# The diagonal of the scores by a select, and a new order of 2000 steps, in a recurrent attention and mixture-of-experts kernel

## Chip, cores and metric

The kernel runs on one core of a Trainium2 chip. The metric is the device time in microseconds (us) of one execution; smaller is better. Times of the trace are counted from the start of its span. TensorE (PE), VectorE (DVE), ScalarE (ACT) and GpSimd (POOL) each work through an instruction queue of their own in order; SP issues most of the DMA transfers, in order as well.

## The reference

Three layers follow each other. The first is a recurrence over 768 time steps with a state of 48x48 for each of 4 batches and 8 heads, the second a feed-forward layer with a softmax and a layer norm between its products, and the third a top-1 mixture of 8 experts.

```python
for t in range(S):                       # S = 768
    cur = np.einsum('bhd,bhe->bhde', u[None] * kt, vt)
    y[:, :, t] = np.einsum('bhd,bhde->bhe', rt, state + cur)
    state = wt[:, :, :, None] * state + np.einsum('bhd,bhe->bhde', kt, vt)
...
h = x @ w_in                             # x: 3072 x 384, w_in: 384 x 1024
solu = h * softmax(h)
ln = (solu - mu) / np.sqrt(var + 1e-06) * g_ln
x = ln @ w_out                           # 1024 x 384
...
expert_idx = np.argmax(x @ w_gate, axis=1)
out[mask] = gate_w[mask, None] * (np.maximum(x[mask] @ w1[e], 0.0) @ w2[e])
```

The term with `u` is the share of the current time step: a number for each token and head, the sum over d of r * u * k.

## The kernel before

The 3072 tokens are cut into 24 units (6 chunks of 128 time steps, for each of 4 batches). In a unit the recurrence becomes products of matrices.

- `plan_T` prepares a unit: it transposes w, r and k on TensorE (`transposes`, L686), takes running products of the decay on VectorE (L700), their inverse on ScalarE (ln and exp, L710 and L712) with a Newton step on GpSimd (`tq` L717, `newt` L721 and L722), and scales r and k with them (`rt` L705, `kt` L727). The diagonal of the scores comes from r * u * k (`ru`, L732 and L733, GpSimd), its sum per head (`a0`, L738, VectorE, 128x8) and `dg` (L743, GpSimd), which spreads the eight sums of a token on the diagonals of eight 128x128 matrices, the tile `am` of 128x1024.
- `plan_A` transposes the scaled k back (`back`, L795, and a copy on ScalarE, L800), makes the scores (L762), copies them under the causal mask over `am` (L766, the diagonal stays as `dg` left it), multiplies with the state and with v (L780), copies the result x into a high and a low half (L785, L788) and brings the state forward (L807, L813, L815, L820).
- `plan_M` is the first product of the MLP with its softmax and norm (L186, L187 and L189; each product is made of three, with high and low halves of both factors), `plan_C` transposes and `plan_O` makes the second product. The MLP of a unit runs seven units behind its attention (LAG = 7); M0 means unit 0's first product, T7 the preparation of unit 7, and so on.
- Before M0 the weights w_in (six pieces of 128x512) and w_out (eight of 128x384) are turned from 64-bit words into 32-bit floats on the chip: load (L221), three steps of integers on VectorE (L226, L228, L229), two checks on ScalarE (L235, L236), a copy as the high half on ScalarE (L243), and the rest as the low half on GpSimd (L244). `prep_gate` folds w_out with the gate's weights (L256, L259, L263), and the result is split as the gate columns (L267 on ScalarE, L268 on VectorE); M0's output takes the same PSUM banks that these columns lay in.
- `gate_steps` picks the expert of each token, and an indirect DMA on GpSimd (L958) scatters the rows into `xsd`, sorted by expert. The experts then work in eight jobs of fixed size: SP gathers rows (L1235), TensorE transposes them (L1244), ScalarE and VectorE split them (L1246, L1247), and both layers of the expert follow (L186 to L189, L1253, L1254, L195). Weights are split into halves on ScalarE and GpSimd (L1046, L1047). The result goes out by an indirect DMA (L1273).

Nothing is issued at once: `at(t, fn)` puts each step on a list, and when all 2000 are there, `emit` runs them in the order of the tuple `_ORDER`, a permutation written out at the head of the file:

```python
def emit():
    steps = sorted(plan, key=lambda x: (x[0], x[1]))
    assert len(steps) == len(_ORDER)
    for q in _ORDER:
        steps[q][2]()
```

A step issues one or several instructions, mostly on one engine; so `_ORDER` sets the order of the queue of each engine and of SP, and nothing else does. A wait of an instruction holds all that stand behind it on its engine. Loads of units have three buffers each (NB = 3): the load of unit 9's w waits until unit 6's transposes have read it.

Some steps by their number: 351 `newt` of T6; 359 `ru` of T7; 353 `kt` of T6; 362 `back` of unit 6; 377 the k transposes of T7; 255 the last L263; 358 the scores of unit 6; 384 its L807; 378 its L780; 408 the r transposes of T8; 381 the copy of x of unit 6 (L785); 341, 345 and 357 the three ScalarE steps of the last piece of w_in (L235, L236, L243); 388 and 389 the gate columns (L267, L268); 392 M0; 395 and 396 the loads of unit 9's w and r; 452 the load of unit 10's v.

Of the kernel before, what the change touches and what calls it, by code (L numbers as in the profile page):

```python
# [13 lines left out]
ALU = mybir.AluOpType  # L14
# [105 lines left out]
def rwkv_moe_kernel(ctx: ExitStack, tc: tile.TileContext, r, k, v, w, u, w_in, w_out, g_ln, w_gate, w1, w2, out, dbg=None):  # L120
    nc = tc.nc
# [566 lines left out]
    def plan_T(i, t, mode):  # L688
# [52 lines left out]
        def dg():  # L741
            u["am"] = aw2.tile([128, 2, 4, 128], F32, tag="am", name="am")
            nc.gpsimd.tensor_tensor(  # L743
                out=u["am"].rearrange("p q a t -> p (q a) t"), in0=ident.rearrange("p (o t) -> p o t", o=1).to_broadcast([128, H, 128]),
                in1=u["a0"].rearrange("p q (a o) -> p (q a) o", o=1).to_broadcast([128, H, 128]), op=ALU.mult)
# [647 lines left out]
```

## Time and profile before

| | before |
|---|---|
| device time, three runs | 671.34, 671.69, 673.26 us (median 671.69) |
| the profiled execution, its own time | 671.95 us |
| its span in the trace | 670.04 us |
| busy: TensorE, VectorE, ScalarE, GpSimd | 626.2, 358.8, 340.1, 386.9 us |
| mean granted clock of TensorE | 0.965 |

A span is the time from the first to the last instruction of the trace; what lies between it and the execution's own time is ahead of or behind it. The execution has four stages: the start, 0 to 97 us, in which the weights are prepared and seven units of attention run ahead; the mixed stretch of attention and MLP, 97 to 430; a short change-over at 430 to 440; and the experts, from there to 670. [...]

### The profile page before, as it was taken

The page shows a single profiled execution, that of the slowest core. Times are in us where ns is not written, and L with a number is a line of the kernel's source. Part 1 is how long each engine was busy: PE and PEld are TensorE (multiplying, and loading weights), DVE is VectorE, ACT ScalarE, POOL GpSimd, SP SyncE. Part 2 cuts the span into 40 slices and gives each one's busy share as a digit, 9 for nine tenths or more (in the row PEclk, how much of TensorE's full clock was granted, in tenths as well). Part 3 has the DMA queues.
Part 4 walks back from the last instruction along what each step waited for, and adds up shares of the span by engine and source line. Part 5 has one row for each costly group of instructions (what it writes and reads, how often), then busy time and mean ns, then how long its engine had stood idle before and what let it go on. Part 6 is the DMA issues. An engine that isn't in the chain of part 4 may idle for free. (4 is left out here: it accounts for less than half of the span.)

```text
span 670.0 us, 13443 instructions
## 1 busy us (share of the span) xinstructions
PE 626.2 (93%) x5143; PEld 569.4 (85%) x5143; DVE 358.8 (54%) x876; ACT 340.1 (51%) x711; POOL 386.9 (58%) x389
## 2 busy tenths in 40 slices
PE   5768689999999999999999999799999999999993
PEld 5657568888888888888888899798999999999993
DVE  7989866785776777686656675432122211131220
ACT  3756645565665555565447785154533534354330
POOL 7888867755369576646600453243756486475541
PEclk8878969999999999999999999989999999999998
DMA  8955611366134122530103121364444455534401
GB/s 194 232 135 127 154 36 36 96 195 198 36 94 109 49 61 48 131 72 25 38 1 102 60 99 51 107 187 151 144 153 131 154 150 166 166 113 152 129 11 35
DMA packets 125103, 72.56 MB, mean 108 GB/s; under 512 B 104071, under 2 KB 115836, under 8 KB 125029
## 3 DMA queue, kind: packets, MB, share of 16 engines
q1 hardware_dynamic: 121749, 62.13, 34.6%
q0 software_dynamic: 3280, 9.47, 3.8%
q8 instruction: 43, 0.70, 0.4%
q14 instruction: 31, 0.25, 0.1%
HBM read 55.79 MB, written 16.29 MB: 108 GB/s over the span
## 5 line engine op out<-in xcount | busy, mean ns | idle before, releaser
L1254 DVE SCALAR_TENSOR_TENSOR hl<-bank,hh 128x384 fp32r<-128x384 f32 (+5 forms) x70 | 37.1, 551 | 112.5 <-ACT hh L1253 103.4
L1047 POOL TENSOR_TENSOR wbl<-stg,wbh 128x768 fp32r<-128x768 f32 x32 | 59.0, 1852 | 36.5 <-ACT wbh L1046 36.3
L195 PE MATMUL bank<-wbh,hh 128*128 128x384 f32 (+4 forms) x216 | 73.7, 341 | 0.0
L195 PE MATMUL bank<-wbl,hh 128*128 128x384 f32 (+4 forms) x216 | 72.6, 336 | 0.0
L186 PE MATMUL bank<-xth,wah 128*128 128x384 f32 (+5 forms) x210 | 71.1, 344 | 0.0
L187 PE MATMUL bank<-xtl,wah 128*128 128x384 f32 (+5 forms) x210 | 69.9, 338 | 0.0
L186 PE MATMUL bank<-wbh,lh 128*128 128x392 f32 x192 | 67.8, 353 | 0.3 <-ACT xo L870 0.3
L1253 ACT ACTIVATE hh<-bank 128x384 fp32r<-128x384 f32 (+5 forms) x70 | 33.1, 490 | 66.0 <-PE bank L189 56.8
L187 PE MATMUL bank<-wbl,lh 128*128 128x392 f32 x192 | 65.2, 340 | 0.0
L1047 POOL TENSOR_TENSOR wal<-stg,wah 128x1024 fp32r<-128x1024 f32 x24 | 57.5, 2407 | 11.6 <-ACT wah L1046 11.4
L717 POOL TENSOR_TENSOR tq<-qe,yq 128x512 f32<-128x512 f32 x24 | 29.1, 1212 | 60.7 <-ACT yq L712 49.8
L1273 POOL DMA_INDIRECT out_dram<-yo,xg x28 | 27.6, 985 | 56.9 <-ACT yo L1270 37.4
L743 POOL TENSOR_TENSOR am<-ident,a 128x1024 f32<-128x1024 f32 x24 | 46.1, 1919 | 4.1 <-DVE a L738 2.8
L189 PE MATMUL bank<-xth,wal 128*128 128x384 f32 (+5 forms) x210 | 47.9, 337 | 0.0
L958 POOL DMA_INDIRECT xsd<-xo,ai x24 | 24.3, 1011 | 37.6 <-DMA xsd<-xo,ai 13.1
L186 PE MATMUL pair<-wah,wah 128*128 128x512 f32 x102 | 42.0, 411 | 2.5 <-DVE wbl L268 2.2
L395 DVE TENSOR_TENSOR ll<-bank,lh 128x512 fp32r<-128x512 f32 x48 | 32.6, 684 | 20.7 <-ACT lh L391 19.1
L195 PE MATMUL bank<-wbh,hl 128*128 128x384 f32 (+4 forms) x216 | 42.1, 336 | 0.0
L186 PEld LDWEIGHTS bank<-xth,wah 128*128 128x128 f32 x210 | 40.3, 192 | 1.3
L187 PEld LDWEIGHTS bank<-xtl,wah 128*128 128x128 f32 x210 | 40.3, 192 | 1.1
L187 PE MATMUL pair<-wal,wah 128*128 128x512 f32 x102 | 40.6, 398 | 0.0
L358 ACT ACTIVATE cc<-s,nmu 128x1024 f32<-128x1024 f32 x24 | 27.6, 1149 | 25.5 <-DVE nmu L356 25.3
(236 smaller groups left out, 1664.6 us busy)
## 6 DMA issues: line engine op xcount, KB each, us to landing
stg<-in_moe_w_dram SPq DMA_DIRECT2D x32, 384.0 KB, 3.3
stg<-in_moe_w_dram SPq DMA_DIRECT2D x24, 512.0 KB, 4.0
xsd<-zrow SPq DMA_DIRECT2D x16, 386.0 KB, 4.7
xg<-xsd SPq DMA_DIRECT2D x24, 193.0 KB, 2.8
lw<-in_w_dram SPq DMA_DIRECT2D x24, 192.0 KB, 3.5
lr<-in_r_dram SPq DMA_DIRECT2D x24, 192.0 KB, 4.1
lk<-in_k_dram SPq DMA_DIRECT2D x24, 192.0 KB, 3.7
lv<-in_v_dram SPq DMA_DIRECT2D x24, 192.0 KB, 3.3
```

What stands on the lines that cost most here:

```text
L186: nc.tensor.matmul(o, ah, bh, start=(i == 0), stop=False)
L187: nc.tensor.matmul(o, ah, bl, start=False, stop=False)
L189: nc.tensor.matmul(o, al, bh, start=False, stop=(i == n - 1))
L195: nc.tensor.matmul(o, a, b, start=(i == 0), stop=(i == len(seq) - 1))
L358: nc.scalar.activation(out=u["cc"], in_=u["s"], func=AF.Identity, bias=u["nmu"])
L395: yield 1.05 + 0.55 * g, lambda g=g, gs=gs: nc.vector.tensor_tensor(out=u["ll"][:, gs, :], in0=lp[g], in1=u["lh"][:, gs, :].bitcast(F32), ...
L717: nc.gpsimd.tensor_tensor(out=u["tq"], in0=u["qe"][:, :, 1:129], in1=u["yq"], op=ALU.mult)
L743: nc.gpsimd.tensor_tensor(out=u["am"].rearrange("p q a t -> p (q a) t"), in0=ident.rearrange("p (o t) -> p o t", o=1).to_broadcast([128, H ...
L1047: at(t + c1, lambda: eng.tensor_tensor(out=dl(), in0=u["st"], in1=dh().bitcast(F32), op=ALU.subtract))
L1253: at(t + d1, lambda: nc.scalar.activation(out=P2["h", 0][:, f, cs], in_=hp, func=AF.Relu))
L1254: at(t + d2, lambda: nc.vector.scalar_tensor_tensor(out=P2["h", 1][:, f, cs], in0=hp, scalar=0.0, in1=P2["h", 0][:, f, cs].bitcast(F32), o ...
L1273: nc.gpsimd.indirect_dma_start(out=out, out_offset=bass.IndirectOffsetOnAxis(ap=xg(j, i)[0:n, XW - 1:XW].bitcast(I32), axis=0), in_=box["y ...
```

## The change

`dg` no longer multiplies the identity with the sums. It selects: where the column t equals the partition, the sum is taken, elsewhere a zero is written. The operation reads one input (`a0`, broadcast along t) instead of two and stays on GpSimd:

```diff
         def dg():
             u["am"] = aw2.tile([128, 2, 4, 128], F32, tag="am", name="am")
-            nc.gpsimd.tensor_tensor(
-                out=u["am"].rearrange("p q a t -> p (q a) t"), in0=ident.rearrange("p (o t) -> p o t", o=1).to_broadcast([128, H, 128]),
-                in1=u["a0"].rearrange("p q (a o) -> p (q a) o", o=1).to_broadcast([128, H, 128]), op=ALU.mult)
+            nc.gpsimd.affine_select(
+                out=u["am"].rearrange("p q a t -> p (q a) t"), in_=u["a0"].rearrange("p q (a o) -> p (q a) o", o=1).to_broadcast([128, H, 128]),
+                pattern=[[0, H], [1, 128]], compare_op=ALU.is_equal, fill=0.0, base=0, channel_multiplier=-1)
         at(o("a0") + 0.1, dg)
```

All of `_ORDER` is replaced by another permutation of the same 2000 numbers; 1862 of them stand in another place, most by a few places, step 395 by 183. Some of the lines with the steps named above:

```diff
 _ORDER = (
...
-    91, 277, 155, 279, 230, 258, 282, 263, 235, 278, 310, 248, 280, 298, 290, 303, 207, 395, 253, 313, 200, 320, 170, 259, 295, 234, 308, 177, 336,
...
-    222, 329, 326, 276, 266, 268, 342, 352, 344, 351, 288, 355, 285, 356, 353, 291, 297, 269, 287, 349, 226, 227, 302, 232, 361, 377, 328, 311, 350,
-    312, 314, 363, 241, 315, 301, 255, 366, 362, 289, 370, 318, 376, 358, 321, 375, 384, 365, 408, 367, 378, 330, 335, 341, 332, 346, 383, 381, 398,
-    345, 450, 382, 357, 374, 388, 161, 389, 360, 392, 385, 379, 364, 380, 386, 402, 401, 409, 112, 410, 404, 400, 411, 111, 416, 333, 413, 414, 403,
...
+    222, 351, 226, 329, 344, 355, 359, 227, 285, 232, 352, 291, 297, 301, 287, 241, 363, 200, 368, 374, 349, 302, 255, 371, 366, 353, 372, 356, 328,
+    449, 362, 311, 377, 450, 350, 373, 312, 314, 318, 321, 376, 388, 315, 358, 397, 370, 365, 384, 339, 332, 333, 367, 378, 346, 375, 330, 383, 408,
+    381, 335, 341, 345, 389, 382, 357, 379, 360, 392, 385, 364, 361, 380, 386, 402, 401, 111, 400, 410, 404, 409, 112, 411, 416, 144, 166, 413, 403,
+    414, 61, 407, 420, 445, 424, 167, 417, 415, 387, 390, 437, 393, 428, 441, 429, 217, 419, 425, 423, 218, 422, 426, 452, 434, 427, 421, 395, 369,
+    455, 396, 442, 439, 430, 433, 459, 405, 438, 440, 431, 454, 467, 468, 456, 446, 457, 462, 500, 469, 406, 460, 436, 483, 435, 484, 472, 443, 391,
...
```

On each queue this makes, around the end of the start and behind it: on TensorE, 362 directly behind 255 and ahead of 377 (before: 377, 255, 362), and 378 ahead of 408 (before behind it); on ScalarE, 388 ahead of the last steps of the weights (before behind 357), and 381 ahead of 341 (before behind it); on GpSimd, 351 ahead of 359 (before behind it); on VectorE, the last integer step of the fourth piece of w_in ahead of 353 (before behind it); on SP, the load of the fifth piece of w_in ten places earlier, and 395 and 396 fifteen and eight places later, now behind 452. In the experts' change-over the first hidden layers of job 0 are issued ahead of the transposes of job 1. After M2 the queue of TensorE is the same but for shifts of a few places.

## Rows read from the trace of the kernel before

**Rows 1.** Windows by stage: length, busy us (instructions) by engine, PEclk, DMA share, GB/s.

```profile
0.00:97.00 97.00, 69.47 (x847) 59.79 (x848) 80.51 (x142) 54.31 (x127) 77.05 (x102) 0.84 0.63 148
97.00:430.00 333.00, 331.60 (x3008) 293.15 (x3007) 230.04 (x636) 190.21 (x417) 180.66 (x211) 1.00 0.30 79
430.00:440.00 10.00, 5.92 (x30) 5.03 (x29) 1.70 (x6) 1.79 (x4) 0.97 (x1) 0.74 0.74 236
440.00:657.00 217.00, 217.00 (x1251) 209.54 (x1251) 46.55 (x93) 93.22 (x163) 127.23 (x75) 1.00 0.43 135
```

**Rows 2.** Windows: the end of the start.

```profile
80.00:97.00 17.00, 11.55 (x117) 9.87 (x118) 13.36 (x22) 9.49 (x24) 10.42 (x9) 0.69 0.18 51
```

**Rows 3.** The waits of TensorE, 410 to 450 us: us in total, times, longest.

```profile
PE bank L1244 <- DMA xg<-xsd: 4.1, 2, 3.2
```

**Rows 4.** Lines of GpSimd, 0 to 97 us: count, busy us, mean ns, idle before.

```profile
L743 POOL TENSOR_TENSOR am<-ident,a 128x1024 f32<-128x1024 f32 x7 | 13.8, 1972 | 0.8 <-PE bank L780 0.8
```

**Rows 5.** Durations of three lines, 0 to 97 us, ns min/median/max.

```profile
L743 POOL TENSOR_TENSOR am<-ident,a x7: 1889/1891/2342, 16.3 to 68.6; 128x1024 f32<-128x1024 f32 x7
...
L721 POOL TENSOR_SCALAR tq<-tq x8: 617/797/1058, 12.0 to 90.6; 128x512 f32<-128x512 f32 x8
...
L226 DVE TENSOR_SCALAR t<-stg x14: 341/872/2053, 5.2 to 84.9; 128x384 int32<-128x384 int32 x8, 128x512 int32<-128x512 int32 x6
```

**Rows 6.** Timeline at 14 us: start, length, engine, line, operation, tiles.

```profile
14.09 1.00 POOL L732 TENSOR_TENSOR ru<-lr,ub 128x384 f32<-128x384 f32 x1
14.20 1.30 DVE L229 SCALAR_TENSOR_TENSOR a<-stg,a 128x384 uint32<-128x384 uint32 x1
```

**Rows 7.** Lines of GpSimd, whole run: a select and the smallest copy.

```profile
L140 POOL TENSOR_SCALAR_AFFINE_SELECT ident<-onesf 128x128 f32<-128x128 f32 x1 | 0.3, 283 | 0.0
...
L872 POOL COPY xo<-tokid 128x1 int32<-128x1 int32 x24 | 4.3, 187 | 0.1
```

**Rows 8.** Timeline of TensorE, 84 to 97 us; in brackets the idle time before.

```profile
84.47 1.11 PE L686 MATMUL bank<-ident,lk 128*128 128x128 f32 x4 [2.41 <-DVE kt L727]
...
85.38 1.29 PE L263 MATMUL pair<-wgt,wT 128*128 128x8 f32 x6
...
86.52 1.09 PE L795 MATMUL bank<-ident,kt 128*128 128x128 f32 x4
...
90.58 1.12 PE L686 MATMUL bank<-ident,lr 128*128 128x128 f32 x4
...
92.90 1.30 PE L780 MATMUL bank<-am,lv 128*32 128x128 f32 x32
...
96.41 0.50 PE L186 MATMUL pair<-wah,wah 128*128 128x512 f32 x1 [2.20 <-DVE wbl L268]
```

**Rows 9.** The timeline of GpSimd, VectorE and ScalarE, 76 to 96 us.

```profile
76.24 1.34 POOL L733 TENSOR_TENSOR ru<-ru,lk 128x384 f32<-128x384 f32 x1
...
80.25 1.24 DVE L226 TENSOR_SCALAR t<-stg 128x512 int32<-128x512 int32 x1 [0.88 <-DMA stg<-in_moe_w_in_dram]
...
84.34 0.68 DVE L229 SCALAR_TENSOR_TENSOR a<-stg,a 128x512 uint32<-128x512 uint32 x1
...
94.29 0.48 ACT L785 CAST wah<-bank 128x384 fp32r<-128x384 f32 x1 [4.97 <-PE bank L780]
...
95.89 0.21 ACT L267 CAST wbh<-pair 128x64 fp32r<-128x64 f32 x1
```

**Rows 10.** The timeline of TensorE in the gap, 437 to 439 us.

```profile
437.60 0.90 PE L1244 MATMUL bank<-ident,xg 128*128 128x128 f32 x3 [0.88 <-DMA xg<-xsd]
...
438.16 0.56 PE L186 MATMUL bank<-xth,wah 128*128 128x256 f32 x1
```

**Rows 11.** A load on SP and a transpose (timeline), and DMA issues.

```profile
111.69 0.37 SPq L680 DMA_DIRECT2D lv<-in_v_dram  x1
...
118.99 0.66 PE L686 MATMUL bank<-ident,lw 128*128 128x128 f32 x4
...
lw<-in_w_dram SPq DMA_DIRECT2D x14, 192.0 KB, 3.4
```

143 rows, old and new, of the table _ORDER are left out of this document.

## The prediction

> **What bounds the kernel now.** I read the windows first, because the share of the whole span hides stages with different limits. From 97 to 430 us TensorE is busy for 331.60 of 333 us, from 440 to 657 for all of 217, both at a granted clock of 1.00 [rows 1]. In those 550 us no other engine and no transfer is late, so an edit there is worth something only if it changes TensorE's own work, and this one doesn't: the same matmuls stand in the new list. What can give is the start (TensorE busy 69.47 of 97 us, clock 0.84) and the ten microseconds from 430 to 440 (5.92 busy, clock 0.74) [rows 1]. [...] Second I read the waits of TensorE: behind 410 us only the gathered rows of the first expert are late, 4.1 us in two waits [rows 3].
>
> Third: who fills the start? GpSimd is busy for 77.05 and VectorE for 80.51 of 97 us [rows 1], and they hold each other up. The sign is in the durations: the conversion step L226 takes 341 ns at best and 2053 at worst, L721 617 to 1058, though neither changes its tile that much [rows 5]. In the timeline a GpSimd product and a VectorE step start 0.11 us apart (14.09 and 14.20), and both take long [rows 6]. So a microsecond of GpSimd in the start is in part a microsecond of VectorE as well, and L743, the line of the change, stands seven times in this stretch, 13.8 us [rows 4].
>
> **The select.** The product of 128x1024 takes 1889 to 2342 ns, with a median of 1891 [rows 5]. The trace has no select of this size. It has one of 128x128 at 283 ns, and the smallest copy on GpSimd at 187 ns [rows 7]. Upper bound: eight such selects, 8 x 0.283 = 2.26 us, dearer than the product. Lower bound: 187 ns fixed, and (283 - 187)/127 = 0.76 ns for each element after the first, 0.187 + 1023 x 0.00076 = 0.96 us. Nearest in kind is L721, also with one input, at best 617 ns for 512 elements [rows 5]: twice that is 1.23 us. I take 1.3, near that row, so 0.6 us off each. Seven of them lie ahead of the first unit of the MLP: 7 x 0.6 = 4.2 us of GpSimd, with the bounds 7 x 0.93 = 6.5 us saved and 7 x 0.37 = 2.6 us lost. GpSimd is busy for 79% of this stretch [rows 1], and part of what it saves turns into idle time; I let three quarters reach the end: **-3.1 us** (-6.5 to +2.6). The other 17 lie under the full TensorE of 97 to 430 us, where GpSimd is busy for 180.66 of 333 [rows 1], and are worth nothing.
>
> [...]
>
> **The order at the end of the start.** The end of the start is the first matmul of unit 0's MLP (M0, L186) at 96.41, after 2.20 us without work; it waits for the split of the gate columns on VectorE (L268) [rows 8], which follows ScalarE's copy of them (L267) at 95.89 [rows 9], since M0 writes the bank that these columns are read from. Back along the chain: unit 6's kt frees the bank for T7's transposes, which start at 84.47 after 2.41 us of waiting; L263 at 85.38 and the transposes of `back` (L795) at 86.52 follow; the last product of unit 6 (L780) runs from 92.90 to 94.20 [rows 8]; only then come the copy of x (L785) at 94.29, behind 4.97 us in which ScalarE was idle [rows 9], the rest of the last weight piece (L236, L243), and the gate columns. In the new list:
> - `back` of unit 6 comes directly behind kt, with T7's transposes after it and L263 ahead of both: 86.52 - 84.47 = 2.05 us earlier [rows 8].
> - T8's transposes (1.12 us at 90.58 [rows 8]) go behind L780, which comes earlier by about that: 1.1.
> - The copy of the gate columns stands ahead of the last weight piece and of x on ScalarE. M0 then waits behind T8's transposes only: 1.12 instead of 2.20 us, 1.08 less [rows 8].
> - Ahead of kt, `newt` of unit 6 passes the two products of `ru` of unit 7 on GpSimd (the second takes 1.34 us), and the piece for which VectorE waited 0.88 us is loaded ten places earlier on SP; against that, an L229 of 0.68 us now lies ahead of kt [rows 9]: 0.88 - 0.68 = 0.20.
>
> Together 4.4 us. The whole list ahead of 80 us is changed as well, VectorE and GpSimd collide in it in new places, and I can't follow that to a microsecond; I take two thirds, **-3.0 us** (0 to -4.4). The new place of the copy of x has a price: it is now ahead of all the ScalarE steps of the last weight piece, so this piece waits for L780 and is ready only behind M0's start. I cost that at nothing: the piece belongs to the second half of M0's columns, and the cover is the nine matmuls of the first half; without it M0 would stand for about as long as L785 to L267 takes today, 95.89 - 94.29 = 1.6 us [rows 9].
>
> **The gap at 430.** The chain of scattered rows on GpSimd and the gather behind it stay. But the first hidden layers (L186) of expert job 0 now come ahead of the transposes of job 1, which TensorE awaits for 0.88 us at 437.60 and behind which the first expert matmul starts at 438.16 [rows 10]. 438.16 - 437.60 = 0.56: **-0.6 us** (0 to -1.0, with the part of the work at half clock).
>
> **The transfers.** SP's queue is reordered by up to 25 places. Each load waits in order, so a load moved behind a blocked one waits too: w and r of unit 9 now stand behind v of unit 10, which waits for a product of unit 7 and is issued at 111.69; unit 9's w is transposed at 118.99 and takes 3.4 us to land [rows 11]. 111.69 + 0.4 + 3.4 = 115.5 leaves 3.5 us. I cost it at nothing (0 to +14, below): the cover is the distance between these two.
>
> **The sum.** The profiled execution took 671.95 us, a span of 670.04 and 1.91 around it, 0.26 above the median of the three runs (671.69). 671.95 - 3.1 - 3.0 - 0.6 = 665.25; on the scale of the median **665.0**.
>
> **Rivals.**
> 1. Nothing arrives. The start is a chain through five engines, and GpSimd's gain turns into idle time: VectorE is busy longer (80.51 us [rows 1]) and the select doesn't shorten it unless the collisions shrink. The waits of 2.41 us for kt and 4.97 us for L780 [rows 8, 9] speak for a chain. Then only the gap's 0.6: about 671.
> 2. The select is not cheaper, 2.26 us as eight small ones: +2.6 x 3/4 = +2.0 in the start, the order's gain of 3.0 and the gap's 0.6 against it: about 670.1.
> 3. The select runs as fast as the lower bound or below: 7 x 1.0 = 7 us of GpSimd, three quarters 5.3, and with the order and the gap -8.9: 662.8. [...]
> 4. Slower: SP's queue. If the new places of the loads make w, r and k land after TensorE wants them, each of about 14 units in the full stretch has a wait of 0.5 to 1.0 us, 7 to 14, and TensorE may lose its clock behind each. It decides at 3.5 us: that is how much later than today's 111.69 a blocked load may be issued before unit 9's transposes wait [rows 11]. With 10 us and the gains above: about 675. Against it: the longest wait of the stretch leaves TensorE full today, and 3.5 us is as much as a whole landing.
>
> **How the numbers follow.** This kernel's measurement can tell 0.3%, about 2.0 us: faster is below 669.7, slower above 673.7. Forecast (661.5 to 668.5): 0.52. Rival 3: 0.12. Together 0.64 faster. Rival 1: 0.14, rival 2: 0.08, together 0.22 the same. Rival 4: 0.14 slower. For the range, the low end is every part at its best, -6.5 - 4.4 - 1.0 = -11.9, 659.8; the high end is rival 2 without the order's gain, 671.7 + 2.0 = 673.7. I give 659.5 to 673.5, which leaves out most of rival 4 and a little at the bottom.
>
> **What would show it.** L743's mean on GpSimd: 1.3 against 0.9 or 2.3. The start of the first L186 of M0: about 90 instead of 96.41, of which the part by order is seen between kt of unit 6 and that matmul (84.47 to 96.41 now, 11.9 us [rows 8]), the part by the select in kt's own time. L226's and L721's longest durations should fall. In 97 to 430 TensorE's waits should stay under a microsecond; waits for lw, lr or lk there would be rival 4. A first matmul of M0 that stays at 96 with an idler GpSimd would be rival 1. Wrong altogether would be a start of the same length with a shorter span behind it.

## The result, and the profile after

The changed kernel takes 652.5 us (median of four runs, 650.75 to 655.88) against 671.52 for the kernel before: a ratio of 0.9718, with a 95% interval of 0.9671 to 0.9764, so 19 us less. The forecast was 665.0, and its range ended at 659.5. The place and the sign were right; the gain is almost three times as large as forecast. The profiled execution took 653.84 us, with a span of 651.8.

First the windows by stage, as in [rows 1], cut where the stages of the changed kernel end:

```profile
0.00:80.98 80.98, 62.40 (x845) 53.55 (x845) 73.82 (x140) 54.11 (x127) 71.53 (x100) 0.92 0.75 177
80.98:416.00 335.02, 332.41 (x3018) 294.70 (x3018) 231.54 (x638) 190.67 (x418) 168.51 (x212) 1.00 0.30 80
416.00:420.00 4.00, 2.24 (x12) 1.48 (x12) 1.12 (x2) 2.18 (x4) 0.00 (x0) 0.93 0.88 289
420.00:640.00 220.00, 220.00 (x1267) 212.57 (x1267) 48.50 (x97) 92.63 (x163) 127.97 (x76) 0.99 0.42 136
```

The start is over at 80.98 us instead of 96.41, 15.4 us earlier; in it GpSimd is busy for 71.53 of 80.98 us (88%, before 79% of 97) and VectorE for 73.82 (91%, before 83%), and TensorE's granted clock, the share of its full speed that it was given, is 0.92 instead of 0.84. From 78 to 98 us of the kernel before, in windows of half a microsecond, it is 1.00 or 0.50 but for the windows in which it changes; these are the two levels below. The 16 matmuls of a unit's scores (L762) take 2.08 us at 87.54, within a stretch at 0.50, and 1.16 at 102.33, in the mixed stretch at 1.00. That stretch is as full as before (332.41 of 335.02 us), and the window cut around the change-over to the experts is four microseconds long instead of ten (how much of that lasts is asked further down). Behind the start the span is 570.8 us long, against 573.6.

The select by its own durations (ns, min/median/max; the product in [rows 5] had 1889/1891/2342), and the conversion step on VectorE that answers to its row in the same group:

```profile
L743 POOL TENSOR_SCALAR_AFFINE_SELECT am<-a x7: 1087/1090/1412, 13.9 to 61.4; 128x1024 f32<-128x1024 f32 x7
```

```profile
L226 DVE TENSOR_SCALAR t<-stg x14: 335/471/1333, 6.5 to 73.0; 128x384 int32<-128x384 int32 x8, 128x512 int32<-128x512 int32 x6
```

The select takes 1.09 us at best and in the median, and seven of them take 8.2 us instead of the 13.8 of [rows 4]. The median of L226 fell from 872 to 471 ns and its longest from 2053 to 1333.

The end of the start on TensorE, as in [rows 8]:

```profile
73.10 0.66 PE L795 MATMUL bank<-ident,kt 128*128 128x128 f32 x4 [0.89 <-DVE su L815]
...
78.44 1.05 PE L780 MATMUL bank<-am,lv 128*32 128x128 f32 x32
79.42 0.66 PE L686 MATMUL bank<-ident,lr 128*128 128x128 f32 x4
80.98 0.50 PE L186 MATMUL pair<-wah,wah 128*128 128x512 f32 x1 [0.91 <-DVE wbl L268]
```

From unit 6's transposes back (L795) to M0 it is 7.9 us; in [rows 8] it was 9.9. And the change-over, as in [rows 3, 10]:

```profile
417.10 1.15 PE L1244 MATMUL bank<-ident,xg 128*128 128x128 f32 x6 [1.03 <-DMA xg<-xsd]
...
418.90 0.36 PE L186 MATMUL bank<-xth,wah 128*128 128x256 f32 x1 [0.53 <-ACT xth L1246]
```

TensorE waits 1.03 us for the gathered rows, where it waited 3.2 and 0.88 before, and the transposes of job 1 no longer stand between those of job 0 and the matmuls that follow on them.

### The profile page after: what moved, and what is told of

Its sections match the earlier page's. It is cut to its first block, busy times and chain, and to the rows that moved or that the text cites. A ratio compares the mean times of both kernels' runs of the same rounds, so it can differ in the third digit from the quotient of the medians.

```text
span 651.8 us, 13454 instructions
## 1 busy us (share of the span) xinstructions
PE 617.9 (95%) x5143; PEld 562.8 (86%) x5143; DVE 355.0 (54%) x876; ACT 340.2 (52%) x711; POOL 369.0 (57%) x389
## 5 line engine op out<-in xcount | busy, mean ns | idle before, releaser
L186 PE MATMUL bank<-xth,wah 128*128 128x384 f32 (+5 forms) x210 | 71.3, 344 | 0.6 <-ACT xth L1246 0.5
L186 PE MATMUL bank<-wbh,lh 128*128 128x392 f32 x192 | 67.7, 353 | 0.5 <-ACT hh L1253 0.5
L186 PE MATMUL pair<-wah,wah 128*128 128x512 f32 x102 | 41.4, 406 | 1.2 <-DVE wbl L268 0.9
L186 PEld LDWEIGHTS bank<-xth,wah 128*128 128x128 f32 x210 | 40.2, 191 | 2.2 <-ACT xth L1246 0.6
L195 PEld LDWEIGHTS bank<-wbh,hh 128*128 128x128 f32 (+4 forms) x216 | 39.3, 182 | 0.9
L195 PEld LDWEIGHTS bank<-wbl,hh 128*128 128x128 f32 (+4 forms) x216 | 39.4, 182 | 0.8
```

The lines of the kernel that those rows point to most:

```text
L186: nc.tensor.matmul(o, ah, bh, start=(i == 0), stop=False)
L195: nc.tensor.matmul(o, a, b, start=(i == 0), stop=(i == len(seq) - 1))
```

## Experiments

The kernels are made from the two lists. Any list in which each pair of steps stands in the order of the old or of the new list keeps what the steps depend on, so the lists could be cut, and single steps moved. All times are ratios to the kernel before, run on the same chip. "M0" is the start of L186 of unit 0's MLP in the profiled execution, "GpSimd busy" its busy time ahead of that, and "idle" the rest.

| kernel | ratio, 95% interval | M0, us | GpSimd busy | idle |
|---|---|---|---|---|
| before | 1 | 96.41 | 76.46 | 19.95 |
| select alone | 0.9994 (0.9968 to 1.0019) | 96.65 | 70.70 | 25.95 |
| order alone | 0.9862 (0.9803 to 0.9920) | 87.20 | 77.81 | 9.39 |
| both (the change) | 0.9718 (0.9671 to 0.9764) | 80.98 | 71.53 | 9.45 |
| both, again | 0.9730 (0.9666 to 0.9794) | 79.30 | 71.33 | 7.97 |
| new until M0 | 0.9725 (0.9668 to 0.9783) | 82.75 | 71.28 | 11.47 |
| new behind M0 | 0.9964 (0.9945 to 0.9984) | 97.53 | 71.08 | 26.45 |
| new until unit 1 | 0.9948 (0.9928 to 0.9967) | 93.99 | 70.95 | 23.04 |
| new until unit 4 | 0.9870 (0.9846 to 0.9894) | 86.38 | 71.86 | 14.52 |
| new from unit 4 on | 0.9847 (0.9796 to 0.9898) | 89.02 | 70.41 | 18.61 |

Each M0 is that of one execution. Where the new list stands up to M0 together with the select it came at 79.30, 80.98 and 82.75 us, so by M0 alone a difference of less than about 3 us between two rows isn't told. TensorE's clock is in it too: for the same matmuls TensorE is busy for 68.9 us ahead of M0 in the kernel before, 71.6 with the select alone, 63.2 with the order alone and 60.9, 62.4 and 65.9 in the three starts just named, with granted clocks from 0.82 to 0.92 in those starts whose windows are shown. What part of an earlier M0 is work at the upper level instead of the lower one, and what part fewer waits, no run here separates.

### The two halves of the change

Select alone: the old list with the new `dg`. Order alone: the new list with the old `dg`.

```diff
-            nc.gpsimd.tensor_tensor(
-                out=u["am"].rearrange("p q a t -> p (q a) t"), in0=ident.rearrange("p (o t) -> p o t", o=1).to_broadcast([128, H, 128]),
-                in1=u["a0"].rearrange("p q (a o) -> p (q a) o", o=1).to_broadcast([128, H, 128]), op=ALU.mult)
+            nc.gpsimd.affine_select(
+                out=u["am"].rearrange("p q a t -> p (q a) t"), in_=u["a0"].rearrange("p q (a o) -> p (q a) o", o=1).to_broadcast([128, H, 128]),
+                pattern=[[0, H], [1, 128]], compare_op=ALU.is_equal, fill=0.0, base=0, channel_multiplier=-1)
```

> The select at L743, the order of before. Order theory (the list itself brings the gain, because the old one let TensorE wait in the middle of the start): the select shortens GpSimd by 7 x 0.8 = 5.6 us ahead of M0, but the waits stay; M0's first matmul at 92 to 95 us (96.41 before), 667 to 670. Lock theory (the shorter select frees GpSimd and VectorE from each other, and this is most of the gain): M0 at 87 or earlier, 662 or less.

Measured: 673.19 us, no change. The windows row of its start:

```profile
0.00:96.65 96.65, 71.64 (x846) 60.97 (x846) 76.95 (x141) 54.30 (x127) 70.70 (x102) 0.82 0.63 148
```

and what GpSimd waits for ahead of M0 (us in total, times, longest), the four largest:

```profile
POOL tq L717 <- ACT yq L712: 5.3, 4, 2.0
POOL wal L244 <- ACT wah L243: 4.1, 2, 3.8
POOL ru L732 <- DMA ub<-in_u_dram: 4.1, 1, 4.1
POOL St L820 <- DVE xs L788: 2.2, 1, 2.2
```

Ahead of M0 GpSimd works 5.8 us less than in the kernel before (70.70 against 76.46), and M0 starts 0.24 us later: all that the select saves turns into waiting. The waits are spread over many places, and each of these is for another engine or a load. VectorE, whose own steps are the same, is busy for 3.0 us less as well (76.95 against 79.92), but this doesn't reach M0 either.

> The new order, the product at L743 as before. Order theory: most of the gain is here; against the changed kernel seven products of 1.89 instead of 1.09 to 1.41 us lie ahead of M0, so M0 at 83 to 87 us, 655 to 659. Lock theory: M0 at 89 or later, 662 or more.

Measured: 664.18 us, M0 at 87.20. The windows row, and what GpSimd waits for ahead of M0:

```profile
0.00:87.20 87.20, 63.21 (x846) 54.06 (x846) 78.51 (x140) 53.74 (x126) 77.81 (x100) 0.90 0.70 164
```

```profile
POOL tq L717 <- DVE a L229: 3.5, 1, 3.5
POOL wal L244 <- ACT wah L243: 1.3, 1, 1.3
POOL tq L717 <- DVE kt L727: 0.4, 1, 0.4
```

Now GpSimd is busy for 77.81 of 87.20 us, 89%, and of the large waits one is left, 3.5 us that end at 8.15 us. Against this kernel the select takes 6.28 us of GpSimd's work away (77.81 to 71.53), and M0 comes 6.22 us earlier (87.20 to 80.98): here about all of it arrives, though that the two numbers meet so closely is luck, given the spread of M0. How it arrives can be followed in part. By the kt of unit 6 the run with the product is 3.0 us behind (74.92 against 71.90). Then VectorE waits for one of GpSimd's low halves (L244), the low half of unit 5's x (L788) comes behind that, and the scores of unit 6 wait for it, where the changed kernel has 0.35 us (74.54):

```profile
78.42 1.77 DVE L228 SCALAR_TENSOR_TENSOR a<-stg,t 128x512 int32<-128x512 int32 x1 [1.18 <-POOL wal L244]
```

```profile
80.71 2.08 PE L762 MATMUL bank<-rt,kt 48*128 48x128 f32 x16 [3.50 <-DVE wal L788]
```

Both theories were wrong as they stood: each expected a gain from the select alone, and the order alone has its M0 next to the order theory's range (83 to 87) but its 664.18 us among the lock theory's times (662 or more). The order brings 9.2 us by itself and the select none, but the two together bring 15.4: the new order takes away waiting, and only with that does less work on GpSimd bring M0 nearer. In the times, 0.9994 x 0.9862 = 0.9856 is what the halves would give by themselves, and 0.9718 is measured; the rest, 1.4%, is 9 us, by the three intervals about 4 to 15. By the profiled executions six of them are ahead of M0, and some of the others can be seen behind it: with the product TensorE waits for unit 7 and those behind it (us in total, times, longest),

```profile
PE bank L795 <- DVE kt L727: 2.9, 2, 2.3
PE bank L762 <- DVE su L815: 1.5, 2, 1.0
```

where the changed kernel waits 1.0 us for the second and not at all for the first.

### Where in the start the order gains

Cut lists, all with the select: the new list up to a step and the old one from there, or the other way round.

```diff
-_ORDER = OLD
+head = NEW[:NEW.index(145) + 1]
+_ORDER = head + [q for q in OLD if q not in head]
```

145 is unit 1's L780 ("until unit 1"). "Until unit 4" has 300, unit 4's L780, and "until M0" 392; "from unit 4 on" (300) and "behind M0" (392) have OLD and NEW exchanged.

> Select at L743; the new order up to unit 1's last product (L780), the old one behind. In the changed kernel that product ends only 0.8 us earlier than before (36.6 against 37.4), though GpSimd is 4 us further on. If the stretches add up, the old order from there on takes what it took, and M0 comes at 95 to 96 us, 670 to 673. If GpSimd's lead carries on through the old order, 91 to 93.

> Select; the new order up to unit 4's last product (58.5 us in the changed kernel, 68.5 before), the old one behind. If the stretches add up: 58.5 + the 28.0 us that the old order took from there to M0 = 86.5, and the total about 10 less than with the select alone, 662 to 664. If the old end lets the lead run into its own waits (the loads of the last weight pieces, which before came at 75 and 76 us): M0 at 89 to 93, 665 to 670.

> Select; the old order up to unit 4's last product, the new one behind it. If the stretches add up: 68.9 (with the select in the old order) + 22.5 = 91 us for M0, against 96.65; and behind M0 the new order's change-over to the experts, 1 instead of 4 us of waiting: 663 to 667 in all. If the end's gain needs GpSimd's lead from the middle: M0 at 94 to 96, 668 to 671.

> The changed kernel, but only the steps up to M0's first product stand in the new order; all behind them stand in the old one. If the whole gain lies in the start (15.4 us by the start of M0), M0 at 81 us, and behind it the old waits of TensorE at the expert change-over (3.2 and 0.9 us) come back: 654 to 657. If the old order behind M0 doesn't fit the new start, TensorE waits in the mixed stretch, and it is over 659.

> Select; the old order up to M0's first product, the new one behind it. M0 at 96.65 as with the select alone. If the shorter change-over to the experts belongs to the steps behind M0: TensorE waits 1 us there instead of 4, 669 to 671. If it comes only with the earlier start: 672 to 674, as with the select alone.

Measured (table above): up to unit 1 the new order brings 96.65 - 93.99 = 2.7 us, between unit 1 and unit 4 93.99 - 86.38 = 7.6, and from there to M0 86.38 - 80.98 = 5.4. These three add up by the way they are taken; the run from unit 4 on, with the old list ahead, is a check of its own, and gives 96.65 - 89.02 = 7.6 for the end. In the times the two cuts at unit 4 do add up: 1.2% and 1.5% below the select alone, against 2.8% for the change. GpSimd's work is the same 70.4 to 71.9 us in all of these; what falls is its idle time, from 25.95 to 9.45. Behind M0 the new list brings little: with the old start the ratio goes from 0.9994 to 0.9964, which the intervals don't tell apart, and the run with the old list behind the new start (0.9725) can't be told from the change.

Of what was expected, M0 of the run until unit 4 fits stretches that add up (86.5); by M0 the run until unit 1 lies between its two ranges, and the run from unit 4 on is better than both of its. The run until M0 has TensorE's old waits for the gathered rows back, 4.0 us in all, as expected; the run behind M0 has 2.6 us there, neither the 1 nor the 4 of its two cases.

### What the middle waits for

Half of the order's gain lies in the middle, of which the forecast said nothing. In the trace of before there is one long wait of TensorE there: T4's k transposes stand for 4.47 us until kt is ready, and unit 2's scores behind them:

```profile
43.27 1.11 PE L686 MATMUL bank<-ident,lk 128*128 128x128 f32 x4 [4.47 <-DVE kt L727]
```

So the scores and L807 were put ahead, in the kernel before:

```diff
-    152, 252, 206, 196, 124, 216, 148, 264, 176, 371,
+    152, 176, 196, 252, 206, 124, 216, 148, 264, 371,
```

252 are T4's k transposes, 176 unit 2's scores, 196 its L807.

> The kernel before (old order, product at L743) with two steps of TensorE moved: the scores of unit 2 (L762, before at 47.66) and its L807 (at 44.31) are issued ahead of the k transposes of T4, which wait 4.47 us for kt. Nothing else. Blocked-queue theory: the scores run at 38 to 40 us, unit 2's L780 ends 6 to 9 us earlier than its 54.0, and a good part of that reaches M0: M0 at 88 to 92, 662 to 667. Throughput theory (GpSimd and VectorE are full and only their work counts): the gain is lost on the way, M0 at 95 to 97, 669 to 672.

Measured: 671.98 us, a ratio of 0.9961 (0.9932 to 0.9989), M0 at 97.20 us. TensorE in this run:

```profile
44.46 1.16 PE L762 MATMUL bank<-rt,kt 48*128 48x128 f32 x16 [2.33 <-DVE wal L788]
...
46.54 1.12 PE L686 MATMUL bank<-ident,lk 128*128 128x128 f32 x4 [0.32 <-DVE kt L727]
```

The scores wait in their new place too, 2.33 us, now for the low half of unit 1's x on VectorE (L788), which stands behind six conversion steps there; and unit 2's L780 comes at 53.41, no earlier than before (52.96). The wait of TensorE was real, but moving what stood behind it is worth little by itself: 0.4% by the times (0.1 to 0.7), and nothing that shows in M0.

The run with the new list until unit 1 shows more. Up to 37 us it does the same as the run with the new list until unit 4, and then it falls back. ScalarE, VectorE and GpSimd there:

```profile
38.27 0.59 ACT L800 COPY ks<-bank 128x512 f32<-128x512 f32 x1 [1.86 <-PE bank L795]
...
39.12 0.50 ACT L785 CAST wah<-bank 128x384 fp32r<-128x384 f32 x1
...
42.69 0.48 ACT L813 COPY su<-bank 128x384 f32<-128x384 f32 x1 [2.62 <-PE bank L807]
```

```profile
39.65 0.56 DVE L788 TENSOR_TENSOR wal<-bank,wah 128x384 fp32r<-128x384 f32 x1 [2.69 <-ACT wah L785]
40.13 0.55 DVE L738 TENSOR_REDUCE a<-ru 128x8 f32<-128x384 f32 x1
```

```profile
40.75 1.00 POOL L732 TENSOR_TENSOR ru<-lr,ub 128x384 f32<-128x384 f32 x1 [1.94 <-DVE a L738]
...
45.09 1.18 POOL L717 TENSOR_TENSOR tq<-qe,yq 128x512 f32<-128x512 f32 x1 [1.03 <-ACT yq L712]
...
54.90 0.51 POOL L820 TENSOR_TENSOR St<-su,qe 64x192 f32<-64x192 f32 x1 [3.15 <-ACT su L813]
```

and TensorE:

```profile
36.04 0.65 PE L780 MATMUL bank<-am,lv 128*32 128x128 f32 x16 [1.73 <-DVE am L766]
...
37.17 1.06 PE L795 MATMUL bank<-ident,kt 128*128 128x128 f32 x4
...
41.32 0.66 PE L686 MATMUL bank<-ident,lk 128*128 128x128 f32 x4 [0.52 <-DVE kt L727]
41.91 0.67 PE L807 MATMUL bank<-lv,ks 128*64 128x48 f32 x16
```

Unit 1's L780 ends at 36.69. Its copy of x on ScalarE (L785) could follow, but `ks` of unit 2 (L800) stands ahead of it and waits 1.86 us for transposes that TensorE makes afterwards; so L785 comes at 39.12. VectorE stands for 2.69 us at the low half (L788), and behind this stands a0 of T3 (L738), which GpSimd's next `ru` needs: 1.94 us of waiting on GpSimd. One step that is a place or two too early on ScalarE goes through three engines. T4's k transposes on TensorE then hold back L807 (41.91), this holds ScalarE for 2.62 us, and GpSimd the next time. This is read from the trace; three edits on this base try it:

```diff
-    209, 180, 185, 293, 123, 115, 158, 191, 202, 190, 160, 215, 224,
+    209, 185, 158, 180, 293, 123, 115, 191, 202, 190, 215, 160, 224,
```

This is A: on ScalarE 158 (the copy of unit 1's x) goes ahead of 180 (`ks` of unit 2) and of 123 (a copy of L259), on VectorE 215 (a0 of T3) ahead of 160 (the low half of unit 1's x). B is on TensorE: 176 and 196 ahead of 252 as above, and 199 (unit 2's L780) with two state steps on GpSimd that it needs (231, 249) ahead of 228 (unit 3's `back`):

```diff
-    152, 252, 206, 196, 124, 216, 148, 264, 176, 371, 257, 181, 183, 195, 153, 156, 219, 229, 233, 149, 242, 228, 251, 231, 150, 249, 174, 261, 237, 163, 199, 267,
+    152, 176, 196, 252, 206, 124, 216, 148, 264, 371, 257, 181, 183, 195, 153, 156, 219, 229, 233, 149, 242, 231, 249, 199, 228, 251, 150, 174, 261, 237, 163, 267,
```

> The same base with the steps on ScalarE and VectorE alone. Blocked-queue theory, where each wait is followed by the next one: GpSimd's wait at 40.75 goes, but T4's k transposes still hold unit 2's scores on TensorE; M0 at 92.5 to 94. If the copy of x is the cause of all: 88 to 91.

> The same base with the steps on TensorE alone (and the two of unit 2's state). The scores of unit 2 wait for bank and copy of x of unit 1 anyway, so they come at 40 to 41 instead of 44 to 45; M0 at 92 to 94 if each wait is followed by the next one, 88 to 91 if TensorE's queue is the cause of all.

> As the run with the new order up to unit 1 (M0 at 93.99 us there), with five steps of the old order's middle put where the new one has them: on ScalarE the copy of x of unit 1 (L785) ahead of unit 2's ks (L800), on VectorE a0 of T3 (L738) ahead of the low half of x of unit 1 (L788), on TensorE the scores of unit 2 (L762) and its L807 ahead of T4's k transposes and its L780 ahead of unit 3's back (with two GpSimd steps of unit 2's state). Blocked-queue theory: GpSimd's waits at 40.75 (1.94 us) and 45.09 (1.03 us) go, unit 2's L780 ends at 43 to 46, and 3 to 6 of the 7.6 us that the middle costs reach M0: 88 to 91. If what the middle costs is spread over all of it, M0 at 92 to 94.

| kernel | ratio, 95% interval | M0, us | idle of GpSimd |
|---|---|---|---|
| new until unit 1 | 0.9948 (0.9928 to 0.9967) | 93.99 | 23.04 |
| with A | 0.9880 (0.9832 to 0.9928) | 90.47 | 18.37 |
| with B | 0.9936 (0.9909 to 0.9962) | 92.14 | 20.85 |
| with A and B | 0.9874 (0.9827 to 0.9921) | 89.60 | 18.05 |
| new until unit 4 | 0.9870 (0.9846 to 0.9894) | 86.38 | 14.52 |

A moves two steps by a place or two on their queues and brings 3.5 of the 7.6 us by M0, 0.7% by the times (0.2 to 1.2); the expectation had given an M0 of 88 to 91 to the case where the copy of x is the cause of all, and 3.5 of 7.6 isn't all. B brings 1.9 us by the start of M0, within its spread, and by the times nothing that can be told; both together bring 4.4, and by the times can't be told from A. GpSimd's waits of 30 to 70 us with both:

```profile
43.38 1.18 POOL L717 TENSOR_TENSOR tq<-qe,yq 128x512 f32<-128x512 f32 x1 [1.25 <-ACT yq L712]
...
63.13 1.09 POOL L743 TENSOR_SCALAR_AFFINE_SELECT am<-a 128x1024 f32<-128x1024 f32 x1 [3.09 <-PE bank L780]
65.25 1.19 POOL L717 TENSOR_TENSOR tq<-qe,yq 128x512 f32<-128x512 f32 x1 [1.02 <-DVE kt L727]
```

The one at 40.75 is gone, and so is that of 3.15 us at 54.90. The one of 1.03 us at 45.09, which was expected to go, is still there (1.25 us at 43.38), and a wait for TensorE at 63.13 has grown from 1.59 to 3.09. The other 3.2 us of the middle lie in later places that weren't taken apart.

### The forecast's own edits at the end

The old list with the select, and the moves that the forecast counted between kt of unit 6 and M0:

```diff
-    361, 377, 328, 311, 350, 312, 314, 363, 241, 315, 301, 255, 366, 362, 289, 370, 318, 376, 358, 321, 375, 384, 365, 408, 367, 378, 330, 335, 341, 332, 346, 383, 381, 398, 345, 450, 382, 357, 374, 388, 161,
+    361, 328, 363, 241, 301, 255, 366, 362, 377, 311, 350, 312, 314, 289, 318, 376, 321, 450, 374, 388, 315, 370, 358, 375, 384, 365, 367, 378, 408, 330, 335, 341, 332, 346, 383, 381, 398, 345, 382, 357, 161,
```

> Select and the old order, with the forecast's edits at the end of the start alone: unit 6's transposes back (L795) ahead of T7's k transposes, unit 6's L780 ahead of T8's r transposes, ScalarE's copy of the gate columns (L267) ahead of the last steps of the weights, and what these need. The forecast's sum: 2.05 + 1.1 + 1.08 = 4.2 us, M0 at 92.4 instead of 96.65, 667 to 669. Idle theory (in the old order GpSimd stands idle for 26 us ahead of M0 and the end has 7 of them; a few edits there give only the part that isn't waiting for VectorE and the loads): M0 at 94 to 95.5, 669 to 672.

Measured: 669.13 us, 0.9924 (0.9899 to 0.9948), against 0.9994 for the select alone: 0.7%, 4.7 us (2.3 to 7.1 by the intervals). In the profiled execution M0 starts at 95.82, only 0.8 us earlier, outside both ranges, and the span behind it is 1.1 us shorter. TensorE in this run, and below it with the select alone:

```profile
86.36 1.09 PE L795 MATMUL bank<-ident,kt 128*128 128x128 f32 x4
...
88.24 2.08 PE L762 MATMUL bank<-rt,kt 48*128 48x128 f32 x16
...
95.82 0.50 PE L186 MATMUL pair<-wah,wah 128*128 128x512 f32 x1 [0.64 <-DVE wbl L268]
```

```profile
86.12 1.09 PE L795 MATMUL bank<-ident,kt 128*128 128x128 f32 x4
87.15 2.08 PE L762 MATMUL bank<-rt,kt 48*128 48x128 f32 x16
...
96.65 0.50 PE L186 MATMUL pair<-wah,wah 128*128 128x512 f32 x1 [2.20 <-DVE wbl L268]
```

Unit 6's kt comes 1.4 us later in this run (84.80 against 83.38 us; VectorE waits 0.6 us longer for the load of a weight piece ahead of it, and that piece's first step takes 0.6 us longer). From the end of kt to M0 it is 10.35 us instead of 12.60: 2.25 less, where the forecast's three items are 4.2. By item: kt to the scores 0.3 instead of 2.05, because T7's k transposes, now behind `back`, still stand ahead of the scores, and L263 ahead of `back` waits 1.76 us for ScalarE; T8's transposes 1.1, as forecast; L780 to M0 0.9, of 1.08. The times agree with the whole 4.2; the trace of this one execution shows half of it in its place, and where the rest of the times' gain lies stays open.

### Is GpSimd the bound now?

If the work of GpSimd makes up the new start, less of it should shorten it further. Two ways, on the changed kernel:

```diff
-        yield lambda: nc.gpsimd.tensor_tensor(out=wil[:, kk, ns], in0=a, in1=wih[:, kk, ns].bitcast(F32), op=ALU.subtract)
+        yield lambda: nc.vector.tensor_tensor(out=wil[:, kk, ns], in0=a, in1=wih[:, kk, ns].bitcast(F32), op=ALU.subtract)
```

> The changed kernel with the low half of w_in (L244, 128x512) on VectorE instead of GpSimd, in the same place of the order. If GpSimd's own work is the bound of the new start (71.5 us busy, 9.5 idle ahead of M0): five of these ahead of M0 at 1.45 us are 7.3 less, M0 at 74 to 76, 645 to 648. If GpSimd and VectorE together are (they hold each other up, and VectorE needs about 0.6 us for each): 5 x 0.85 = 4.2 less, M0 at 76 to 78, 648 to 650. If neither: M0 at 80 to 83, 651 to 655.

```diff
-            nc.gpsimd.tensor_scalar(out=u["tq"], in0=u["tq"], scalar1=-1.0, scalar2=2.0, op0=ALU.mult, op1=ALU.add)
+            nc.scalar.activation(out=u["tq"], in_=u["tq"], func=AF.Copy, scale=-1.0, bias=2.0)
```

This one is for six of the eight units prepared ahead of M0.

> The changed kernel with the first half of the Newton step (L721, 2 - x, 0.6 to 0.9 us) on ScalarE for six of the eight units that are prepared ahead of M0; the second half (L722) stays where it was on GpSimd, with one other GpSimd step between it and the first product. If GpSimd's own work is the bound: 6 x 0.65 = 3.9 less, M0 at 77 to 78, 647 to 650. If GpSimd now waits for ScalarE, which has its own queue: M0 at 80 to 84, 651 to 656.

> The changed kernel itself, for a comparison on the same chip as the three others: M0 at 80 to 82 us, 651 to 655.

Measured, all on one chip: 0.9761 (0.9718 to 0.9805) and 0.9701 (0.9659 to 0.9743), and the changed kernel beside them 0.9730 (0.9666 to 0.9794, with 657.09 us and M0 at 79.30 beyond its own two ranges): no difference that can be told. The starts of the first two:

```profile
0.00:83.04 83.04, 61.36 (x846) 52.99 (x846) 76.96 (x144) 53.08 (x125) 66.63 (x97) 0.92 0.75 172
```

```profile
0.00:82.21 82.21, 65.99 (x845) 56.74 (x846) 71.83 (x139) 56.40 (x131) 66.56 (x94) 0.85 0.74 174
```

In both GpSimd works 4.9 us less, and M0 comes at 83.04 and 82.21, not earlier than 79.30 to 80.98. So no sign is left that GpSimd's work alone decides once the select is in. With the low halves on VectorE, that engine is busy for 76.96 of 83.04 us, 93%; by the intervals a gain of more than about 3 us is excluded. For the step on ScalarE the answer is weaker. No engine is over 88% there, and the waits are longer (15.65 us of idle GpSimd instead of 8 to 9.5), but its start also had a granted clock of 0.85 instead of 0.92, with TensorE busy for 66.0 us instead of 60.9 to 62.4, and by the intervals of the times a gain of up to some 7 us isn't excluded, so its 3.9 isn't either. That a list fits the durations it was tried with, and a shorter step alone leaves a hole, would explain both; it isn't shown.

## Why the prediction was wrong

Where to look was right. The mixed stretch and the experts' second half had nothing to give and gave nothing; the gain is in the start and the change-over, and it shows in the first L186 of M0, at 80.98 instead of the 90 that were forecast.

The price of the select was near: 1.3 us were taken, between 0.96 and 2.26, and 1.09 in the median, 1.17 in the mean were measured; with that 5.8 us of GpSimd's work went ahead of M0, where 4.2 were forecast. One reading beside it was wrong, without a place in the sum: of the two steps of [rows 6] that "both take long", the GpSimd product's 1.00 us is its usual time (median 999 ns ahead of M0), and only the VectorE step is long (1.30 us; the same step on the same tile takes 0.53 at best).

The first step that failed is "I let three quarters reach the end". The share came from the busy time, as if a part of each saved microsecond arrived whatever stands around it. The runs show nought and all: in the old list GpSimd's 5.8 us become 6.0 us of idle time, in the new list 6.28 us go with an M0 that is 6.22 earlier (up to 7.9 with the second execution). Rival 1 had the mechanism for the select ("GpSimd's gain turns into idle time") and was given 0.14, and its sign, a first matmul of M0 that stays at 96 with an idler GpSimd, is what the select alone shows. The collisions that this rival left open may have shrunk, by the 3.0 us that VectorE is busy for less, and nothing arrived even so: these went into waiting as well. The rows for the rival were there, 20 us of idle GpSimd ahead of M0 and waits of other engines all along.

The second is the term "-3.0 us (0 to -4.4)" for the order. It was worked out for the last 12 us of the start, 4.4, and in its total this was about right for that place: from the end of unit 6's kt to M0 it was 12.0 us before and is 8.4 and 7.2 us in the two executions of the changed kernel. In its parts it wasn't: the 2.05 us for `back` counted T7's k transposes as gone, but they still stand ahead of the scores, and from kt to the scores it is 2.0 us instead of 3.1, 1.2 less; the second execution is shorter from the scores on, which take 1.16 us in it instead of 1.97. But the term stood for the whole list, "changed ahead of 80 us as well", of which the forecast took only that it couldn't be followed, and cut the term by a third. The order brings 15.7 us with the select, 2.7 of them up to unit 1, 7.6 in the middle and 5.4 at the end. The best case of what couldn't be followed belonged into the range: in the kernel before GpSimd stood idle for 20 us ahead of M0 and VectorE for 16, and with the select the new list took GpSimd's idle time from 25.95 to 9.45. The low end of 659.5 counted the select at its best and nothing of these 20 us.

The third is that the terms were added. Select and order are worth 0 and 9.2 us alone and 15.4 together, so a sum of what each is worth alone could not come out right.

The change-over was sized at -0.6 us, and up to -1.0 with part of the work at half clock; the granted clock was 0.50 there from 435 to 441.5 us in the kernel before. In the profiled execution its waits went from 4.1 [rows 3] to 1.0 us, with 0.7 us of smaller ones behind it. The chain of scattered rows and the gather behind it, which were to stay, are shorter there: the gather is issued 3.6 us behind the last scatter, and was 5.0 us behind it. But in a second execution of the changed kernel it is 4.9 us, and TensorE waits 2.82 us, near the 3.2 of [rows 3]:

```profile
419.68 1.14 PE L1244 MATMUL bank<-ident,xg 128*128 128x128 f32 x6 [2.82 <-DMA xg<-xsd]
```

So whether that step failed isn't settled. Over the runs here TensorE waits 3.1 to 4.8 us for these rows with the old list there (ten kernels) and 0.9 to 2.8 with the new one (seven traces), which speaks for the list and not for the earlier start. The span behind M0 was 572.4 to 576.5 us with the old list and 570.1 to 576.2 with the new one, with means of 574.0 and 572.9: about 1 us of the 19 by the means, 2.8 by the first two profiles.

The transfers were rightly costed at nothing. TensorE's waits from 81 to 400 us in the changed kernel, all of them (us in total, times, longest):

```profile
PE bank L762 <- DVE su L815: 1.0, 1, 1.0
PE pair L186 <- DVE wbl L268: 0.9, 1, 0.9
PE pair L186 <- DVE s L350: 0.3, 1, 0.3
```

No load is among them; rival 4 didn't happen, and neither did the last weight piece, costed at nothing, hold M0's second half. Rival 2 is out by the select's price, and rival 3 was nearer to the price (1.09, its 0.9 or below) but put the same three quarters on it.

## What to carry to other kernels

Ahead of the milestone that ends a stage, write down each engine's work and its idle time. Here work taken from an engine that stood idle for a fifth of the stage was worth nothing until the order let it run; the idle time is the most that a new order can give back on that engine; and the two were no sum: each was worth more with the other. Look for steps that stand one place too early on an engine whose input comes late: in the middle of this start one such copy on ScalarE was worth 3.5 us, while TensorE's longest wait, attacked directly, was worth little. And compare one execution's milestone only against the spread of another one of the same kernel.

## What was not expected of the hardware

Beside a select, too, a VectorE step can be long. In the changed kernel a select runs from 13.88 to 15.09 us, and a conversion step (L228, 0.55 us at best) starts within it, takes 1.25 us and ends 0.4 us behind it:

```profile
13.88 1.21 POOL L743 TENSOR_SCALAR_AFFINE_SELECT am<-a 128x1024 f32<-128x1024 f32 x1
```

```profile
14.26 1.25 DVE L228 SCALAR_TENSOR_TENSOR a<-stg,t 128x384 int32<-128x384 int32 x1
```

Ahead of M0 VectorE's steps, the same work in four kernels, take 79.92 us with the product and 76.95 with the select in the old order, 78.51 and 73.82 in the new one: 3.0 and 4.7 us less where GpSimd's steps are shorter. How the one follows from the other, no run here shows. That the shorter select is what shortened L226 isn't shown either: its median is 851 ns with the select alone and 604 with the order alone (872 before, 471 with both), and L228's is 810 before and 808 with both. L721's longest, which was to fall from 1058 ns, is 910 in one execution of the changed kernel and 1067 in the other.

And two executions of one program differ in the start. The changed kernel reached M0 at 80.98 and at 79.30 us, and 1.2 of these 1.7 us lie behind unit 6's `back`: the same scores, behind the same waits (0.9 us for `back`, 0.35 us here), took 1.97 us in one, near the 2.08 of the lower level of the clock, and 1.16 in the other, as at the upper level. The first had a granted clock of 0.50 from 75 to 78 us; over the whole start it is 0.92 in the first and 0.94 in the second.

```profile
74.54 1.97 PE L762 MATMUL bank<-rt,kt 48*128 48x128 f32 x16 [0.35 <-DVE wal L788]
```

```profile
74.06 1.16 PE L762 MATMUL bank<-rt,kt 48*128 48x128 f32 x16 [0.35 <-DVE wal L788]
```

Their spans are 651.8 and 655.5 us, so the one with the earlier start is the longer: its change-over waited 1.8 us longer, and the 50 us around it (379 to 429, in the other 381 to 431) had a granted clock of 0.93 instead of 0.97, and both go with the 5.4 us by which it is longer behind M0; how much each makes isn't taken apart.
